# Linear attention and a gated convolution block on one core: four heads' transposes on TensorE, the feature weights on another queue, and a new order list

## The chip, the cores and the metric

The kernel runs on one core of a Trainium2 chip. A core has TensorE (PE in the profile; PEld is its weight load), VectorE (DVE), ScalarE (ACT), GpSimd (POOL) and SyncE (SP). Each engine works through its own queue of instructions in order and waits on semaphores for the others. Transfers are issued from the queues of SP, ACT and POOL and run on 16 DMA engines. The metric is the device time of one execution in microseconds (us); lower is better. The median of three runs before the change is 225.8 us (225.17 to 226.18).

## The reference

There are 8 batches, 8 heads, 576 tokens and 64 numbers per head. Each token's q and k go through the same 64 x 128 matrix `w_phi`, then exp; the attention is linear (keys times values first), and its output runs through a block with a causal depthwise convolution of 5 taps, a sigmoid gate and two 512 x 512 products.

```python
def phi(x):
    proj = np.einsum('bhsd,df->bhsf', x, w_phi)
    proj = proj - np.max(np.abs(proj), axis=-1, keepdims=True)
    return np.concatenate([np.exp(proj), np.exp(-proj)], axis=-1)
q_p, k_p = (phi(q), phi(k))
kv = np.einsum('bhsf,bhsd->bhfd', k_p, v)
z = np.sum(k_p, axis=2)
num = np.einsum('bhsf,bhfd->bhsd', q_p, kv)
den = np.einsum('bhsf,bhf->bhs', q_p, z)[..., None] + 1e-06
...
gate = 1.0 / (1.0 + np.exp(-gate_pre))   # gate_pre: causal convolution of x with conv_w
val = x @ w_val
return (gate * val @ w_out).astype(np.float32)
```

## The kernel before, in words

**Units.** The work is cut into 40 units. Units 0 to 31 are pairs of heads: unit 4b+hp holds heads 2hp and 2hp+1 of batch b, without the last 64 tokens. Units 32 to 39 are the tails: unit 32+b holds the last 64 tokens of all heads of batch b. PSUM has 8 banks, and each operation that writes one names it.

**The order list.** What each engine does, and when, is written out by hand in the string `ORDER` (line 31 on). A word such as `XP.30@5` or `XX.30:A` names an operation, its unit, the PSUM bank after `@` and the engine after `:` (A is ACT, D is DVE, P is POOL). The loop at line 929 calls the function `op_...` of each word in turn, and every engine gets its instructions in that order. So the list sets the order in the five queues, the banks, and for copies the engine too. The words that matter here:

- `LD` (line 364) loads a piece of k, q or v of one batch from POOL's queue; `LD.0` and `LD.1` bring k and q of the second pair of heads of batch 0, `LD.2` and `LD.3` those of the third and fourth. The first pair comes by SP's and ACT's queues (lines 189 to 198), with `w_phi` into the tile `wtmp` between its k and its q.
- `CK`, `CQ`, `W`, `WB` copy that first pair and `w_phi` to bf16 tiles (`W2`, and `W2Z` with zeros beside it).
- `T` (line 368) transposes q and k of a unit on TensorE, `TX` the q half of unit 0; `C` and `CX` copy the result from PSUM to the tile `T`.
- `PK` and `PA` (lines 448, 455) multiply k and q with `w_phi` for the maxima; `MA`, `MB`, `MK`, `MQ` take these maxima on DVE; `KA`, `KB`, `K0`, `K1` take exp of k on ACT (lines 532 and 590). `PQ`, `SA` and `XA`, `XB`, `X0`, `X1` do the same for q, with the maximum subtracted in PSUM by a matmul; `MT` and `MC` turn that maximum round for it.
- `V` scales the values on POOL, `KV` and `KM` form and copy keys times values, `N` and `XN` (lines 686, 713) multiply with q and divide. The result, the tile `XN`, has tokens on the partitions.
- `XP` (line 733) turns `XN` round, channels on the partitions, into the batch's tile `XT`. Without a bank it is a transposing transfer by the crossbar on SP's queue (line 745). With a bank it is four 128 x 128 transposes on TensorE (line 751), and `XX` (line 753) copies them from PSUM to `XT`. The tails always take TensorE.
- `HL` (line 760) copies the four halo planes of `XT` that the convolution reads, `GF` (line 791) is the convolution of a batch on TensorE, `GT` that of its tail, `TH` the tanh, `VA` and `VB` (lines 817, 821) the product with `w_val`, `GV` the gating, `OA` and `OB` (lines 834, 843) the product with `w_out`, `OE` its copy out of PSUM, `ST`, `SL` and `SU` the stores on SP's queue. `FL` is a matmul on zeros whose result nobody reads.

```python
if bank is None:
    nc.sync.dma_start_transpose(
        xt(u.b)[:, u.hp, 4 * 64:12 * 64].rearrange("p (c t) -> p c t", t=P), xf,
    )
else:
    u.XPps = PS[:, bank[0], 0:256].bitcast(BF16)
    for c in range(4):
        nc.tensor.transpose(u.XPps[:, c * P:(c + 1) * P], xf[:, c * P:(c + 1) * P], ident_bf[:, :])
```

Before the change only the last batch (units 28 to 31) has its `XP` with a bank; the other 28 units go by the crossbar.

Of the kernel before, what the change touches and what calls it, by code (L numbers as in the profile page):

```python
# [36 lines left out]
MT.2@4 MC.2:D C.7:D XA.3 T.5@3 C.5:D SA.2 KB.3 E.2 LD.8 V.32:P XA.2 PQ.1@5,4 PA.4@6,7 MQ.4 SA.1 V.2:P PK.4@0,2
MB.4 XB.1 MA.4 T.33@6,7 C.33:D XB.2 KB.4 XA.1 PA.5@3,4 MQ.5 KA.4 KV.1@1 KV.0@7 LD.22 KM.1:D V.3:P LW.0 KM.0:D
PK.33@2,3:W MK.33 MT.4@1 MC.4:D T.6@5 C.6:A N.0@6,7 MQ.33 XN.0 XP.0 N.1@0,1 XN.1 K1.33 K0.33 PK.5@5,4 PA.7@6,7
MQ.7 KB.5 PQ.4@2,3 KA.5 KV.2@0 KM.2:D SA.4 XA.4 MB.5 TP.0@1 CW.0:D E.33 XB.4 N.2@6,7 PQ.33@0,1:W MA.5 KV.3@4  # L40
SA.33 XN.2 XP.2 PK.6@2,5 E.4 XP.1 KM.3:D T.8@6 MT.7@7 MB.6 C.8:D X1.33 X0.33 N.3@3,4 KB.6 XN.3 CV.3:P CV.2:P
XP.3 PK.7@1,0:W MA.7 MC.7:D N.32@6 PA.6@4,5 XN.32 CV.0:P CV.1:P MQ.6 DG.0:P DF.0:P V.33:P KA.6 PQ.7@3,7 SA.7
FL.7@6 V.5:P DF.2:P DF.3:P KA.7 XA.7 XP.32@6 XX.32:D MA.6 DF.1:P T.9@1 C.9:D XB.7 HL.0:P MT.5@4 T.11@6 MC.5:D
KB.7 C.11:D PA.8@2,3 MQ.8 PK.8@1,5:W KA.8 PQ.5@7,4 LD.11 SA.5 XA.5 KV.5@6 MB.7 E.6 XB.5 V.6:P GT.0@2,3 VT.0
KM.5:D MA.8 GF.0@0,1,6,7 HT.0 LD.13 MB.8 LW.1 V.4:P CO.1:P KB.8 TH.1 GW.0 MT.6@4 MC.6:D T.34@2,3 C.34:D TH.0
N.5@4,5 XN.5 XP.5 PK.34@2,3:W PA.9@6,7 K1.34 LD.12 K0.34 MQ.9 PQ.6@4,5 SA.6 V.7:P XB.6 CO.3:P MQ.34 T.10@0
C.10:D PK.9@7,6:W KV.6@1 MK.34 XA.6 MA.9 MT.8@5 KV.4@0 KM.6:A N.6@2,3 MB.9 MC.8:A KM.4:A XN.6 XP.6 N.4@0,1
XN.4 KA.9 XP.4 PQ.8@7,4 PK.10@2,3 KB.9 MA.10 CO.2:A E.8 V.9:P SA.8 V.8:P PA.11@5,6 MQ.11 XA.8 MB.10 VA.2@0
KV.7@1 KM.7:A VB.2 GV.2 VA.3@7 N.7@5,6 XN.7 XP.7 KA.10 XB.8 KB.10 VB.3 GV.3 VA.1@0 LD.14 PA.10@1,2 MQ.10
PK.11@5,6 LD.18 VB.1 GV.1 KB.11 N.33@7 XN.33 PQ.34@3,4 SA.34 VA.0@2 MT.11@1 E.34 X0.34 MC.11:A MB.11 T.13@0  # L50
C.13:D X1.34 KA.11 VB.0 GV.0 T.12@7 C.12:D XP.33@1 XX.33:A LD.16 HL.1:P PQ.11@3,4 SA.11 XA.11 GT.1@0,1 HT.1
MT.9@6 MC.9:D CO.0:P V.34:P MA.11 XB.11 VT.1 E.10 GW.1 V.11:P LD.17 GF.1@2,3,6,7 TH.3 PQ.9@5,4 SA.9 TH.2
PA.12@0,1 XA.9 T.15@6 MQ.12 OA.1@7 PK.12@2,3 KA.12 C.15:D PQ.10@0,1 OB.1 MB.12 XB.9 MT.10@6 V.10:P LD.15
KV.9@5 MC.10:D KM.9:D OE.1:D OA.0@6 SA.10 MA.12 OB.0 KV.8@7 OE.0:D KB.12 KV.11@5 KM.8:D KM.11:D PA.13@2,3
T.35@6,7 N.9@4,5 MQ.13 XN.9 XA.10 XB.10 C.35:A PK.13@0,1 KB.13 PK.35@2,3 MA.13 K0.35 N.8@6,7 XN.8 FL.17@4
FL.18@5 MT.12@4 MC.12:A K1.35 KV.10@5 T.14@4 XP.9 KM.10:A PQ.12@6,7 MB.13 SA.12 MQ.35 MK.35 KA.13 C.14:D
OA.3@5 N.11@0,1 XN.11 N.10@2,3 XN.10 XP.8 XP.11 XP.10 ST.0 XB.12 OB.3 XA.12 OE.3:A PK.15@4,7 PK.14@0,1 KA.14
MA.15 OT.0@6 OF.0:A N.34@5 MA.14 XN.34 PA.15@2,3 OA.2@6 MQ.15 VA.6@0 OB.2 OE.2:D ST.1 KA.15 VB.6 GV.6 MB.14
PQ.35@4,5:W VA.7@2 SA.35 KB.15 E.12 X0.35 X1.35 VA.4@3 VB.7 MT.13@6 MC.13:A VB.4 KB.14 E.35 MB.15 E.14 V.12:P
T.19@0 GV.7 MT.15@4 C.19:D MC.15:D LD.23 GV.4 PQ.13@6,7 SA.13 XA.13 XP.34@2 XB.13 XX.34:D PQ.15@1,0 PA.14@4,5  # L60
MQ.14 SA.15 XA.15 VA.5@3 XB.15 VB.5 LD.19 GV.5 HL.2:P T.16@2 C.16:D GF.2@4,5,6,7 TH.5 PA.16@2,3 GT.2@0,1 TH.4
MQ.16 T.17@6 C.17:D MT.14@7 MC.14:A VT.2 PQ.14@4,3 HT.2 GW.2 PK.16@2,7 PA.17@5,6 KA.16 SA.14 MB.16 MQ.17
OA.5@1 XA.14 OA.4@0 OB.5 V.13:P MA.16 OE.5:D V.14:P OB.4 V.35:P KV.13@6 KM.13:D T.36@4,5 C.36:D T.18@2 KB.16
V.15:P N.13@6,7 C.18:D XN.13 MT.16@5 XB.14 PK.17@4,3 OE.4:A MC.16:A PK.36@0,1 MK.36 KA.17 KV.12@2 XP.13 K0.36
K1.36 OA.7@7 MB.17 LD.25 KV.14@5 OB.7 KM.12:D MA.17 KM.14:A OE.7:A KV.15@2 MQ.36 KM.15:D N.12@4,5 XN.12 KB.17
E.16 PQ.16@1,7 SA.16 XA.16 N.35@6 XP.12 XN.35 N.14@2,3 XB.16 XN.14 ST.2 PQ.36@4,5:W T.20@0 C.20:D SA.36 X0.36
# [10 lines left out]
SA.37 X1.37 X0.37 VA.13@2 VB.14 MT.23@0 MC.23:A GV.14 VB.13 XP.36@6 GV.13 XX.36:D PK.23@7,5 PQ.23@3,4
PA.22@0,1 SA.23 KA.23 MQ.22 MB.23 XA.23 VA.12@2 MA.23 XB.23 OT.1@6 VB.12 GT.4@0,1 GV.12 T.24@3 VT.4 OF.1:D
MT.21@7 KB.23 OA.12@4 T.38@5,6 C.24:D PA.24@2,3 ST.3 E.22 HT.4 MC.21:A GW.4 PQ.21@7,0 MQ.24 SA.21 LD.20 V.20:P
V.37:P V.21:P C.38:A HL.4:P XB.21 OB.12 LD.26 OE.12:D T.25@1 GF.4@2,3,5,6 C.25:D XA.21 TH.9 PK.24@4,0 MA.24  # L80
# [891 lines left out]
```

## Time and profile before

| | before |
|---|---|
| median of the runs | 225.8 us |
| profiled execution, its own time | 226.87 us |
| span of its trace | 225.1 us |
| PE busy | 202.4 us (90%), 3828 matmuls |
| ACT busy | 194.4 us (86%) |
| DVE busy | 184.1 us (82%) |
| POOL busy | 133.4 us (59%) |
| crossbar transposes | 28, all on SP's queue |
| transfers | 31.38 MB, 139 GB/s over the span |

The profiled execution is 1.1 us above the median and 1.8 us above its own span. The views used below: the busy time of each engine in stretches of the span, the chain of waits (followed back from the last instruction, each step to what released it), the timeline of single engines, the groups of instructions by line, and the transfers with their time from issue to landing. The durations of ACT and DVE rows overlap where one instruction follows another closely, so a pair of exps that is 1.1 us long in the timeline moves the chain by 0.98 us.

### The profile page before, as it was taken

To read this page: it belongs to the slowest core of one execution; us is meant where nothing else is said; L and a number is where in the kernel's file an instruction comes from. 1 tells how busy PE (TensorE), PEld (TensorE's weight loads), DVE (VectorE), ACT (ScalarE), POOL (GpSimd) and SP (SyncE) were. 2 spreads that over 40 slices of the span, in tenths; PEclk is the share of its full clock that TensorE was granted. 3 is DMA by queue.
4 is the path that set the end of the run, shared out by engine and by line. 5 is a ranking of instruction groups with operands and counts; after the bars stand their busy time and mean duration, and the time that the engine had idled before them with its cause. 6 is when DMAs were issued, how large, how long until landed. Compare 5 with 4: busy or idle time off the path is not lost.

```text
span 225.1 us, 8971 instructions
## 1 busy us (share of the span) xinstructions
PE 202.4 (90%) x3828; PEld 138.2 (61%) x3854; DVE 184.1 (82%) x337; ACT 194.4 (86%) x425; POOL 133.4 (59%) x172
## 2 busy tenths in 40 slices
PE   0687899996798999999998999999999999999997
PEld 0464677765465665678656775776676666466542
DVE  6499999987886999889996999999988997466341
ACT  3599999998988998999998999999989998777541
POOL 8779967999779702993359509952816086500100
PEclk9997999999999999999999999999999999999999
DMA  5999997699999996984928595796550226304846
GB/s 114 197 199 218 270 203 116 121 204 173 132 167 205 152 147 142 179 141 55 197 50 115 62 203 111 169 136 111 126 114 20 57 47 129 134 4 114 247 105 192
DMA packets 41362, 31.38 MB, mean 139 GB/s; under 512 B 16869, under 2 KB 37349, under 8 KB 41322
## 3 DMA queue, kind: packets, MB, share of 16 engines
q0 software_dynamic: 20816, 14.90, 47.6%
q1 hardware_dynamic: 19882, 15.04, 29.9%
q10 hardware_dynamic: 624, 0.87, 1.2%
q8 instruction: 30, 0.49, 0.9%
q14 instruction: 10, 0.08, 0.1%
HBM read 32.58 MB, written 9.44 MB: 187 GB/s over the span
## 4 chain that ended last, share of the span: by engine, by line
PE 57%; ACT 26%; DVE 9%; issue 3%; DMA 2%; SPq 1%; ACTq 0%; DVEq 0%
PE PS L841 11%; PE PS L812 10%; ACT QT L551 9%; ACT KT L538 8%; PE PS L443 5%; PE PS L706 5%; PE PS L629 4%; PE PS L393 4%; ACT GATE L801 3%; PE PS L652 3%; PE PS L785 3%; PE PS L668 2%; DMA GV<-in_q_dram 2%; DVE MKA L509 2%; PE PS L288 2%
## 5 line engine op out<-in xcount | busy, mean ns | idle before, releaser
L615 POOL TENSOR_TENSOR VT<-vN,EA 128x1024 bf16<-128x1024 bf16 x32 | 61.0, 1907 | 37.2 <-ACT EA L569 30.8
L538 ACT ACTIVATE KT<-PS 128x512 bf16<-128x512 f32 x128 | 70.7, 659 | 2.3 <-PE PS L443 2.2
L551 ACT ACTIVATE QT<-PS 128x512 bf16<-128x512 f32 x128 | 69.2, 657 | 2.8 <-PE PS L668 2.5
L509 DVE TENSOR_REDUCE MKA<-PS 128x4 f32<-128x512 f32 x64 | 42.6, 682 | 1.6 <-ACT KT L538 0.8
L494 DVE TENSOR_REDUCE MQX<-PS 128x8 bf16<-128x1024 f32 x30 | 36.5, 1219 | 4.7 <-PE PS L443 4.4
L812 PE MATMUL PS<-XT,WVAL 128*128 128x512 bf16 x128 | 34.8, 380 | 0.1
L841 PE MATMUL PS<-WOUT,GV 128*128 128x512 bf16 x107 | 30.9, 380 | 1.3 <-issue 0.6
L443 PE MATMUL PS<-W,T 64*128 64x128 bf16 x472 | 24.5, 223 | 4.3 <-ACT T L242 1.8
L828 DVE SCALAR_TENSOR_TENSOR GV<-GATE,PS 128x512 bf16<-128x512 bf16 x32 | 20.9, 680 | 5.3 <-PE PS L812 5.3
L443 PEld LDWEIGHTS <-T 64*128 64x128 bf16 x472 | 15.9, 96 | 12.9 <-issue 6.6
L726 DVE TENSOR_TENSOR XN<-PS,RCPA 128x512 bf16<-128x512 f32 x32 | 22.1, 692 | 1.1
L606 POOL TENSOR_TENSOR VTZ<-vN,EA 64x512 bf16<-64x512 bf16 x16 | 16.6, 1040 | 10.3 <-PE PS L668 6.5
L629 PEld LDWEIGHTS <-KT 128*128 128x128 bf16 x512 | 18.6, 97 | 6.6 <-ACT QT L551 1.2
L629 PE MATMUL PS<-VT,KT 128*128 128x65 bf16 x512 | 21.0, 193 | 1.5 <-ACT QT L551 0.6
L244 POOL COPY XT<-XT 128x1008 bf16<-128x1008 bf16 x8 | 8.2, 1025 | 22.3 <-ACT XT L242 16.1
L706 PEld LDWEIGHTS <-QT 128*128 128x128 bf16 x512 | 18.6, 97 | 4.3 <-issue 0.4
L706 PE MATMUL PS<-KVSA,QT 128*128 128x65 bf16 x512 | 20.6, 193 | 0.1
L244 DVE COPY T<-PS 128x1024 bf16<-128x1024 bf16 x27 | 18.3, 683 | 1.6 <-PE PS L393 1.6
L393 PE MATMUL PS<-ident_bf,kN 128*128 128x128 bf16 x128 | 13.5, 233 | 6.1 <-ACT kN L242 5.5
L801 ACT ACTIVATE GATE<-PS 128x1024 bf16<-128x1024 f32 x16 | 16.0, 1082 | 3.4 <-PE PS L785 3.4
L812 PEld LDWEIGHTS <-WVAL 128*128 128x128 bf16 x128 | 10.5, 97 | 8.4 <-issue 0.6
L852 DVE TENSOR_SCALAR OS<-PS 128x512 f32<-128x512 f32 x16 | 10.9, 685 | 5.5 <-PE PS L841 5.5
(103 smaller groups left out, 371.1 us busy)
## 6 DMA issues: line engine op xcount, KB each, us to landing
out_dram<-OS SPq DMA_DIRECT2D x28, 256.0 KB, 3.6
kN<-in_k_dram POOLq DMA_DIRECT2D x14, 320.0 KB, 7.1
vN<-in_v_dram POOLq DMA_DIRECT2D x14, 320.0 KB, 5.9
qN<-in_q_dram POOLq DMA_DIRECT2D x7, 576.0 KB, 10.8
OS<-in_moe_w_val_dram SPq DMA_DIRECT2D x1, 1024.0 KB, 9.4
out_dram<-OSt SPq DMA_DIRECT2D x8, 128.0 KB, 2.4
vN<-in_v_dram POOLq DMA_DIRECT2D x4, 160.0 KB, 8.0
OS<-in_moe_w_out_dram SPq DMA_DIRECT2D x2, 256.0 KB, 4.4
```

The source lines that it names most:

```text
L244: read(engines[eng].tensor_copy(dst, x), bank)
L443: nc.tensor.matmul(PS[:, bank[par], c0 + blk * P:c0 + (blk + 1) * P], u.T[r, i, blk, :], W2[r, :], start=True, stop=True,)
L494: read(nc.vector.tensor_reduce(MQX[:, i // G % NG, :].rearrange("p (r c) -> p r c", r=2)[:, :, c:c + 4], tokview(u.PA, 0, u, None), AX.X, ...
L509: read(nc.vector.tensor_reduce(out, half_ps(bank, x, out, wide), AX.X, ALU.max, apply_absolute_value=True,), [bank[x]])
L538: read(nc.scalar.activation(out, half_ps(u.PK, x, out, u.PKwide), AF.Exp, scale=1.0 if ft == 0 else -1.0,), [u.PK[x]])
L551: read(nc.scalar.activation(dst, PS[:, u.PQ[x], :].rearrange("p (x t) -> p x t", t=64), AF.Exp, scale=1.0 if ft == 0 else -1.0,), [u.PQ[x]])
L615: e.tensor_tensor(u.VT[:, :, :, 0:D], x.unsqueeze(1).to_broadcast([P, 2, n, D]), w.unsqueeze(3).to_broadcast([P, 2, n, D]), ALU.mult,)
L629: nc.tensor.matmul(PS[:, bank[0], c:c + E1], u.KT[:, ft, j // 2, j % 2, :], u.VT[:, ft, j, :], start=(jj == 0 and x == 0), stop=False, ski ...
L706: nc.tensor.matmul(PS[:, bank[c // 2], x * E1:(x + 1) * E1], u.QT[:, ft, c, h2, :, :].rearrange("p j t -> p (j t)"), kv[:, ft, h2, :], sta ...
L801: read(nc.scalar.activation(m.GATE[q2][:, :, :], banks(*bank), AF.Tanh), bank)
L812: nc.tensor.matmul(PS[:, m.val[jt], :], WVAL[:, dt, jt * P:(jt + 1) * P], planes(xt(m.b), slice(0, P), dt, 4), start=(dt == 0), stop=(dt = ...
L841: nc.tensor.matmul(PS[:, bank, :], lhs(jt), WOUT[:, jt, :], start=(jt == 0), stop=(jt == 3))
```

## The change

Three things change.

1. In the list, `XP.0` to `XP.3` get a bank and `XX.0` to `XX.3` are added: the four pairs of heads of batch 0 are transposed by TensorE and copied to `XT`, one by ACT and three by DVE. 24 crossbar transposes stay.
2. `w_phi` is loaded into `wtmp` from POOL's queue, ahead of everything else there, and no longer from SP's and ACT's queues between k and q of the first pair. On DVE the small tiles made from the identity (`nident`, `ident5`, `id32`) come after the zero fills and no longer between them.
3. The whole list is another one: nearly every word stands elsewhere, and banks differ. Some copies change engine. Of the plain copies out of PSUM, ACT gets six more `OE`, one more `OF`, two more `KM` and the `XX` of two more tails, and loses one `C`, one `CO`, three `MC` and two `XX` of pairs. DVE gets `XX` of six pairs, two `HL`, one `C`, three `MC` and `WB`, and loses six `OE`, one `OF`, two `KM` and two tails' `XX`.

```diff
@@ -29,82 +29,82 @@
 ORDER = """
-LD.0 LD.1 CQ.0:D Z.1:P CK.0:A T.0@5 LD.3 LD.2 W.0:A C.0:A PK.0@0,2 KA.0 TX.0@7 CX.0:A MB.0 T.1@1 C.1:D
...
+CK.0:A T.0@3 WB.0:D LD.1 C.0:D CQ.0:D LD.0 W.0:A PK.0@4,5 KA.0 MB.0 LD.2 LD.3 TX.0@2 CX.0:A LC.0 T.1@6 MA.0
...
@@ -154,6 +154,9 @@
     ctx.enter_context(tc.manual_schedule())
 
+    wtmp = const.tile([P, F], FP32, name="wtmp")
+    for t in range(2):
+        nc.gpsimd.dma_start(wtmp[t * 64:(t + 1) * 64, :], w_phi[:, :])
     ident_bf = const.tile([P, P], BF16, name="ident_bf")
     make_identity(nc, ident_bf[:])
@@ -188,9 +191,6 @@
     W2 = const.tile([P, F], BF16, name="W2")
-    wtmp = const.tile([P, F], FP32, name="wtmp")
-    for t in range(2):
-        (nc.sync, nc.scalar)[t].dma_start(wtmp[t * 64:(t + 1) * 64, :], w_phi[:, :])
     for t in range(2):
@@ -205,14 +205,6 @@
     nc.vector.memset(W2Z[:, :, :].rearrange("p a f -> p (a f)"), 0.0)
-    nc.vector.tensor_scalar_mul(nident[:, :], ident_bf[:, :], -1.0)
-    ident5 = const.tile([5, 5], FP32, name="ident5")
...
@@ -231,6 +223,13 @@
     nc.vector.memset(MQX[:, :, :].rearrange("p g c -> p (g c)"), 0.0)
+    nc.vector.tensor_scalar_mul(nident[:, :], ident_bf[:, :], -1.0)
+    ident5 = const.tile([5, 5], FP32, name="ident5")
...
```

The list's effect is seen in the queues. First POOL's queue at the start of the program, before:

```order
masks.py:199 AFFINE_SELECT ident_bf<-ident_bf 128x128
L178 DMA kN<-in_k_dram 64x2x320 x2
L172 DMA qN<-in_q_dram 128x576
L334 MEMSET OS 128x1
L172 DMA qN<-in_q_dram 128x2x576
L178 DMA kN<-in_k_dram 64x4x320 x2
L244 CAST W2Z<-wtmp 64x128 x2
L178 DMA vN<-in_v_dram 64x4x320 x2
```

and the same place now:

```order
L159 DMA wtmp<-in_w_phi_dram 64x128 x2
masks.py:197 MEMSET ident_bf 128x128
masks.py:199 ISA
masks.py:199 AFFINE_SELECT ident_bf<-ident_bf 128x128
L175 DMA qN<-in_q_dram 128x576
L181 DMA kN<-in_k_dram 64x2x320 x2
L181 DMA kN<-in_k_dram 64x4x320 x2
L175 DMA qN<-in_q_dram 128x2x576
L270 MEMSET VTZ_134 128x1040
L181 DMA vN<-in_v_dram 64x4x320 x2
```

The two transfers of `wtmp` come first, q of the second pair (128x576) passes k of that pair (64x2x320), and k of the third and fourth pair (64x4x320) passes their q. The casts to `W2Z` left POOL for DVE.

Then SP's queue up to the second batch's crossbar transposes, before:

```order
L178 DMA GV<-in_k_dram 64x2x320
L193 DMA wtmp<-in_w_phi_dram 64x128
L195 DMA GV<-in_q_dram 64x576
L291 DMA cw_115<-in_moe_conv_w_dram 5x512
L338 DMA OS<-in_moe_w_val_dram 128x4x512
L745 DMA_TRANSPOSE XT_130<-XN 128x4x128 x4
L343 DMA OS<-in_moe_w_out_dram 32x4x512
L343 DMA OS<-in_moe_w_out_dram 32x2x512 x4
L745 DMA_TRANSPOSE XT_132<-XN 128x4x128 x4
```

and now:

```order
L181 DMA GV<-in_k_dram 64x2x320
L195 DMA GV<-in_q_dram 64x576
L290 DMA cw_115<-in_moe_conv_w_dram 5x512
L337 DMA OS<-in_moe_w_val_dram 128x4x512
L342 DMA OS<-in_moe_w_out_dram 32x4x512
L342 DMA OS<-in_moe_w_out_dram 32x2x512 x4
L744 DMA_TRANSPOSE XT_125<-XN 128x4x128 x4
```

(`GV` is the tile that the first pair's k and q land in; `XT_130` and `XT_123` are the `XT` of batches 0, 2, 4 and 6, `XT_132` and `XT_125` that of the odd ones.) The first four transposes, those of batch 0, are gone from the queue, as is `wtmp`, so that q follows k at once and the load of `w_out` follows that of `w_val`.

Last DVE's queue where batch 0's results are copied into `XT` now:

```order
L725 TENSOR_TENSOR XN<-PS,RCPA 128x512
L243 COPY T<-PS 128x1024
L493 TENSOR_REDUCE MQX<-PS 128x2x4
L243 COPY T<-PS 128x1024
L243 COPY XT_123<-PS 128x512
L508 TENSOR_REDUCE MKA<-PS 128x4
L243 COPY XT_123<-PS 128x512
L243 COPY XT_123<-PS 128x4x64
L243 COPY XT_123<-PS 128x512
```

Three copies of 128x512 stand there that were not in this queue before; the one of 128x4x64 is the tail's and was there.

More of the change, by code (lines that the diff above doesn't have):

```diff
@@ L37 @@
[L37 to L66, printed above, removed]
@@ L77 @@
[L77 to L80, printed above, removed]
-V.22:P OA.13@1 KV.20@7 MB.24 KM.20:D MT.22@5 OB.13 TH.8 V.23:P MC.22:D KV.21@6 PA.25@2,3 OE.13:D KM.21:D MQ.25
@@ L108 @@
+FL.3@4 FL.13@6 FL.10@4 FL.4@3 FL.19@6 FL.21@0 FL.2@2 OE.31:A SL.31
 """
@@ L233 @@
     nc.vector.memset(MQX[:, :, :].rearrange("p g c -> p (g c)"), 0.0)
+    nc.vector.tensor_scalar_mul(nident[:, :], ident_bf[:, :], -1.0)
+    ident5 = const.tile([5, 5], FP32, name="ident5")
+    nc.vector.tensor_copy(ident5[:, :], ident_bf[0:5, 0:5])
+    id32 = const.tile([P, 32], FP32, name="id32")
+    nc.vector.tensor_tensor(id32[:, :], ident_bf[:, 0:32], ident_bf[:, 32:64], ALU.add)
+    nc.vector.tensor_tensor(id32[:, :], id32[:, :], ident_bf[:, 64:96], ALU.add)
+    nc.vector.tensor_tensor(id32[:, :], id32[:, :], ident_bf[:, 96:128], ALU.add)
     MQT = const.tile([P, NG, P], BF16, name="MQT")
```

119 lines of the change are left out of this document (74 added, 45 removed).

## The prediction

> **What bounds the kernel now.** I read the busy time of the engines in stretches first, because the averages of the page (PE 90%, ACT 86%, DVE 82%) hide that different engines are full at different times. Columns: stretch in us, its length, busy us and instructions of PE, PEld, DVE, ACT and POOL, granted clock, transfers' share, GB/s.
>
> ```profile
> core 0: us, PE busy (x) PEld busy (x) DVE busy (x) ACT busy (x) POOL busy (x), PEclk, DMA share, GB/s
> 30.00:35.00 5.00, 4.55 (x104) 3.67 (x102) 4.93 (x12) 5.00 (x11) 1.71 (x4) 1.00 1.30 206
> 35.00:40.00 5.00, 4.60 (x95) 3.66 (x93) 4.90 (x13) 5.00 (x15) 4.77 (x7) 1.00 0.54 79
> 45.00:50.00 5.00, 4.80 (x159) 3.44 (x154) 4.05 (x10) 5.00 (x13) 4.98 (x7) 1.00 1.17 202
> 50.00:55.00 5.00, 3.42 (x78) 2.94 (x74) 3.84 (x7) 4.04 (x10) 5.00 (x6) 1.00 1.30 192
> 55.00:60.00 5.00, 4.56 (x83) 3.22 (x80) 4.82 (x10) 5.00 (x14) 3.37 (x6) 1.00 1.76 147
> 60.00:70.00 10.00, 8.03 (x201) 5.36 (x200) 7.13 (x13) 8.00 (x22) 8.44 (x12) 1.00 1.31 160
> 100.00:110.00 10.00, 9.89 (x225) 7.94 (x226) 9.86 (x22) 9.80 (x23) 5.27 (x7) 1.00 0.68 90
> 110.00:120.00 10.00, 9.95 (x167) 5.99 (x182) 9.77 (x16) 8.59 (x22) 5.13 (x8) 1.00 0.41 83
> 190.00:200.00 10.00, 9.59 (x215) 6.26 (x212) 4.90 (x8) 7.43 (x15) 4.13 (x5) 1.00 0.34 111
> ```
>
> Three stretches follow. At the start the first data and the first copies set the pace (the chain below). In the rows from 30 to 50 us ACT has no idle time and DVE hardly any up to 40, while PE has 0.45 and 0.40 us to spare in five. Later PE is full (9.89 and 9.95 of 10), with ACT close behind. Between the last two, from 50 to 70 us, lies the largest idle time of PE after the start: 1.58 + 0.44 + 1.97 = 3.99 us.
>
> The chain of waits tells what the start hangs on. Columns: start, length, what.
>
> ```profile
> 1.55 0.83 SPq L193
> 2.42 5.33 DMA GV<-in_q_dram
> 7.85 0.47 DVE qN L244
> 8.37 1.48 PE PS L393 x12
> 9.87 0.70 DVE T L244
> ```
>
> The first q is issued behind `w_phi` (0.83 us of SP's queue), lands 5.33 us later, and its copy on DVE, the transposes of q and of unit 1 on PE and the copy of unit 1's result follow without a gap. The timeline names the two longest stalls of PE from 50 to 70 us, by the idle time in brackets and what ended it:
>
> ```profile
> 53.46 0.23 PE L560 MATMUL PS<-ident_bf,MQX 128*128 128x128 bf16 x1 [1.54 <-ACT KVSA L242]
> 61.94 0.46 PE L443 MATMUL PS<-W,T 64*128 64x128 bf16 x10 [1.21 <-issue]
> ```
>
> **The change part by part: the start.** Without `w_phi` between them, q's transfer on SP starts where `w_phi`'s did, 2.42 - 1.55 = 0.87 us sooner, and CQ could run at 6.98. That is the most to win. Against it stands POOL's queue, by these rows (single issues on POOL with their length in ns and their start; PE's first transposes and those of unit 1; time from issue to landing, of the two k pieces and of q behind them):
>
> ```profile
> L178 POOL DMA_DIRECT2D kN<-in_k_dram x1: 776/776/776, 1.4 to 1.4; - x1
> L178 POOL DMA_DIRECT2D kN<-in_k_dram x1: 596/596/596, 2.2 to 2.2; - x1
> 2.80 0.58 POOL L172 DMA_DIRECT2D qN<-in_q_dram  x1
> 5.46 0.61 PE L393 MATMUL PS<-ident_bf,kN 128*128 128x128 bf16 x4 [5.46 <-ACT kN L242]
> ...
> 8.77 0.63 PE L393 MATMUL PS<-ident_bf,kN 128*128 128x128 bf16 x4
> ...
> DMA to landing us min/median/max: 3.6/4.8/5.9
> DMA to landing us min/median/max: 5.8/5.8/5.8
> ```
>
> Two issues for `w_phi`, estimated at the 0.78 + 0.60 of the two for k, and the 0.58 for q now stand ahead of k of the second pair, so its first piece is issued near 1.4 + 1.38 + 0.58 = 3.4 and its second near 4.1 instead of 2.2. With 5.9 us the second lands at 10.0 instead of 8.1; with the 3.6 us of the other piece, at 7.7. Unit 1's transposes, which began at 8.77, need it, and PA.0 and PK.1 are queued behind them on PE; their maxima and exps wait in turn. So the start gains at most 0.87 and loses at most 10.0 - 8.77 = 1.2. The bytes ahead of that piece are the same set as before, only in another order, and the whole set had landed by 2.80 + 5.8 = 8.6; I therefore place unit 1 near 8.4: **-0.4** (ends -0.9 and +1.2). `W` and `WB` need the two `w_phi` transfers, issued near 0.7 and 1.4. With 3.6 to 5.9 us they land between 5.0 and 7.3; the transposes of unit 0 end at 5.46 + 0.61 = 6.1, so this costs nothing up to the middle of that span, and its bad end is inside the +1.2.
>
> **The four transposes.** The group rows and the two queue rows that price them:
>
> ```profile
> L751 PE MATMUL PS<-ident_bf,XN 128*128 128x128 bf16 x16 | 1.5, 219 | 0.0
> L242 ACT ACTIVATE XT<-PS 128x512 bf16<-128x512 bf16 x4 | 2.4, 596 | 0.7 <-PE PS L751 0.5
> L244 DVE COPY Tt<-PS 128x512 bf16<-128x512 bf16 x6 | 2.5, 416 | 0.2 <-PE PS L386 0.2
> 31.98 9.47 SPq L745 DMA_TRANSPOSE XT<-XN  x4
> 44.02 1.02 POOL L244 COPY XT<-XT 128x1008 bf16<-128x1008 bf16 x1
> 44.47 0.74 PE L881 MATMUL PS<-XT,DIAGF 128*128 128x64 bf16 x20
> 38.06 0.69 DVE L726 TENSOR_TENSOR XN<-PS,RCPA 128x512 bf16<-128x512 f32 x1
> ```
>
> PE gets another 16 transposes, 1.5 us busy. They fall between 30 and 45 us, where PE has about 0.4 us idle in five and waits for ACT and DVE: **0** (end +1.5, if that cover is gone). The copies cost ACT 0.60 us and DVE 3 x 0.42 = 1.25 us, in the stretch where both are full. I count the one on ACT, which is full in every row from 30 to 50, and not those on DVE, which has 0.95 us idle right behind, from 45 to 50: **+0.6** (ends 0 and +1.9). What goes is latency: the last division of batch 0 ends at 38.06 + 0.69 = 38.75, its crossbar transposes occupy SP's queue until 41.45, and the halo copy starts at 44.02. By TensorE the same tile is ready near 38.75 + 0.4 + 0.4 = 39.6, some 4 us sooner. PE did not wait for it (the rows of L881 follow without idle time), and the list puts this work behind about as much ACT work as before, so by itself it is worth **0**.
>
> **Copies that change engine.** Their prices, from the groups of instructions:
>
> ```profile
> L850 ACT ACTIVATE OS<-PS 128x512 f32<-128x512 f32 x16 | 9.9, 638 | 3.3 <-PE PS L841 3.3
> L852 DVE TENSOR_SCALAR OS<-PS 128x512 f32<-128x512 f32 x16 | 10.9, 685 | 5.5 <-PE PS L841 5.5
> L242 ACT ACTIVATE MQT<-PS 128x128 bf16<-128x128 bf16 x16 | 5.1, 316 | 2.5 <-PE PS L560 2.4
> ```
>
> Seven output copies move to ACT: 7 x 0.64 = +4.5; three MQT leave: -0.9; the other moves nearly cancel except one T copy and one weight copy less. My total for ACT is about +2.5 us, with batch 0's XX in it; DVE stays within 0.5 us of what it had. Behind 100 us ACT has room (1.41 us between 110 and 120, 2.57 between 190 and 200) and PE is the fuller engine: **0** beyond the 0.6 counted (end +1.9).
>
> **The list.** No row prices a new order. What it can win is PE's idle time, and the two stalls named above, 1.54 and 1.21 us, are of the kind that an order moves: a copy queued behind exps on a full ACT, and a bank that comes free late. SP's queue and `XT` no longer tie batch 0's gate to 44 us, which gives the list PE work to put there. I take one such stall as gone, **-1.4** (ends: +1.4, one more of that size, and -4.0, all of 50 to 70).
>
> **Sum:** -0.4 + 0 + 0.6 + 0 + 0 - 1.4 = -1.2. On the profiled execution, 226.9 us with a span of 225.1, that gives 225.7 and 223.9; the median, 1.1 below it, goes from 225.8 to **224.6**.
>
> **The rivals.**
> - *The list finds more.* If both stalls go and PE's idle time from 60 on shrinks a little, -0.4 + 0.6 - 2.75 - 0.4, near 222.9. For it: four transfers fewer in SP's queue, and data 4 us sooner. Against: from 100 us PE is at 99% already, and its work grows by 1.5.
> - *Nothing comes of it.* Freed latency that nobody waited for: -0.4 + 0.6, 226.0. For it: L881 shows no idle time before it.
> - *Slower by the loads.* The wait for the first q gives way to one for k of the second pair, behind three issues on POOL that were not ahead of it. From a landing later than 8.8 us on, unit 1 is late, and where ACT is full, up to 50 us, such a delay is not caught up: +1.2 + 0.6, 227.6.
> - *Slower by ACT.* If the evictions given to ACT stand where it has no idle time (0.20 us in 10 between 100 and 110), +0.6 + 1.9 - 0.4 = +2.1: 227.9.
> - *Slower by a port.* DVE's zero fills and casts now run while POOL issues `w_phi`. The first of the two k issues above took 0.18 us longer than the second, with DVE's small casts beside it; the longest fill is this:
>
> ```profile
> 2.48 1.12 DVE L227 MEMSET DIAGF<- 128x1280 uint32 x1 [0.19 <-issue]
> ```
>
> If an issue had to wait for a whole fill, 1.1 us would come on top of POOL's queue, and the start would lose 1.1 - 0.4 = 0.7: with the copies +1.3, 227.1. The rule behind this is in the Trainium skill, "SBUF — State Buffer", section "SBUF: two separate sides": transfers issued from GpSimd have their descriptors written by GpSimd, which VectorE locks out while one of its two-port operations runs, and the page advises the other two queues. So it speaks against moving `w_phi`. By the 0.18 us between the two issues the trace agrees at most weakly; no row of it shows a long lock.
> - *That the change does less than it says:* SP's queue in the new order has no transpose ahead of batch 1's, so this has no chance worth a number.
>
> **How the numbers follow.** The sum 0.44, with a range of its own from 223.4 to 225.7; the list finds more 0.18; nothing comes of it 0.15; the loads 0.10; ACT 0.08; the port 0.05. A difference under 0.5%, 1.13 us, cannot be told from none here. Below 224.67 lie 0.26 of the first case and all of the second: faster 0.44. Within 0.5% lie 0.18 of the first, 0.14 of the third and 0.01 of the port: 0.33. The rest, 0.23, is slower. The range for 8 in 10 reaches from the better half of the second case to the loads: 222.3 to 227.5.
>
> **What would show it.** The copy of q (DVE qN) near 7.0 and unit 1's transposes near 8.4 show the start right; transposes at 9.5 or later with the wait put down to the k transfer show the loads. The first halo copy before 42 us shows the latency gone. PE busy from 50 to 70 above 17.4 (16.0 before) shows the term of the list; the same idle time elsewhere shows it wrong. ACT's busy time near 197 us shows the moved copies, and stretches after 100 us with ACT full and PE below 9.5 of 10 would be the fourth rival. A gain that comes after 100 us, where I give none, would make the working wrong even with the right time.

## The result

The changed kernel takes **229.11 us** (median; 229.01 to 229.51) against 225.88 us for the kernel before on the same chip. The ratio is **1.0151**, 95% interval 1.0124 to 1.0178: slower by 3.4 us. In a later set on another chip the same pair gave 1.0127 (1.0086 to 1.0169). The forecast of 224.6 and its range of 222.3 to 227.5 are both wrong.

Times of one kernel spread more in some sets of runs than in others, so below a ratio to the kernel before in the same set is given, without the disturbed runs (six of eleven in experiment 2, five of twelve in experiment 1); a difference in us is that ratio times 225.6 less 225.6.

**The profile after.** Its execution took 229.02 us, with a span of 227.2. First the stretches, with the columns of the prediction:

```profile
core 0: us, PE busy (x) PEld busy (x) DVE busy (x) ACT busy (x) POOL busy (x), PEclk, DMA share, GB/s
45.00:50.00 5.00, 3.18 (x137) 2.71 (x134) 3.19 (x6) 4.19 (x11) 5.00 (x7) 1.00 0.94 206
50.00:55.00 5.00, 4.74 (x118) 3.79 (x102) 4.29 (x8) 4.78 (x9) 4.84 (x8) 1.00 0.91 116
55.00:60.00 5.00, 4.60 (x91) 3.26 (x89) 4.93 (x10) 4.96 (x15) 2.01 (x2) 1.00 0.52 90
60.00:70.00 10.00, 9.79 (x223) 6.86 (x221) 8.30 (x17) 9.63 (x25) 9.64 (x14) 1.00 0.60 74
100.00:110.00 10.00, 9.54 (x207) 7.41 (x209) 8.19 (x18) 8.93 (x23) 3.42 (x5) 1.00 1.18 184
110.00:120.00 10.00, 8.88 (x135) 5.15 (x135) 9.65 (x17) 9.05 (x20) 3.79 (x4) 1.00 0.30 30
```

From 50 to 70 us PE is busy for 4.74 + 4.60 + 9.79 = 19.13 us, where it was 16.01: the stalls that the prediction wanted gone are gone. But from 45 to 50 it has 3.18 instead of 4.80, and from 110 to 120 it has 8.88 instead of 9.95. New idle time stands elsewhere. The groups of instructions say whose it is. Behind the last bar stands the idle time of PE just ahead of the group and what ended it; the first row is of the kernel before, the second of the changed one:

```profile
L892 PE MATMUL PS<-XT,WVAL 128*128 128x64 bf16 x128 | 5.0, 193 | 1.0 <-ACT GATEt L901 0.9
```

```profile
L891 PE MATMUL PS<-XT,WVAL 128*128 128x64 bf16 x128 | 5.0, 193 | 4.3 <-ACT GATEt L900 4.3
```

The group is the operation `VT`: for the last 64 tokens of a batch it multiplies x with `w_val`, 16 matmuls, 0.63 us, in each batch. It has 3.3 us more idle time ahead of it, about what was lost. ACT's `GATEt` is `HT`, the tanh of the same tokens' gate. `GT` (their convolution on PE) fills columns 0 to 127 of two banks, `HT` reads them, and `VT` writes columns 128 to 255 of the same two banks; `GW` on DVE then multiplies both. So `VT` does not need `HT`'s result, yet it waits for it when it stands behind it in the list. Around batch 0 in the timeline of the changed kernel:

```profile
45.69 0.74 PE L880 MATMUL PS<-XT,DIAGF 128*128 128x64 bf16 x20
48.26 0.63 PE L891 MATMUL PS<-XT,WVAL 128*128 128x64 bf16 x16 [1.82 <-ACT GATEt L900]
45.73 2.20 ACT L550 ACTIVATE QT<-PS 128x512 bf16<-128x512 f32 x4
47.64 0.57 ACT L900 ACTIVATE GATEt<-PS 128x256 bf16<-128x256 f32 x1
44.40 1.02 POOL L243 COPY XT<-XT 128x1008 bf16<-128x1008 bf16 x1
```

`GT.0` ends at 46.4. ACT is full and works off four exps first, so `HT.0` begins at 47.64, and PE waits 1.82 us for it with everything that is queued behind. The other waits are 1.00, 0.58, 0.49 and 0.36 us, in batches 3 to 6. The list tells why there are more of them now:

```diff
-GT.0@2,3 VT.0 KM.5:D MA.8 GF.0@0,1,6,7 HT.0
+GT.0@2,3 XB.5 HT.0 VT.0 GW.0 GF.0@0,1,6,7
...
-GT.3@0,1 MQ.20 OE.8:D KA.19 E.18 LD.21 V.17:P V.19:P SA.17 VT.3 HT.3
+GT.3@4,5 HT.3 C.21:D VT.3
```

Before, `HT` stood ahead of `VT` in three of eight batches (1, 5, 7); now it does in seven, all but batch 2.

The start came out nearly as forecast (copy of q, PE's first transposes of unit 1):

```profile
6.64 0.46 DVE L243 CAST qN<-GV 128x576 bf16<-128x576 f32 x1
8.57 0.59 PE L392 MATMUL PS<-ident_bf,kN 128*128 128x128 bf16 x4 [0.76 <-DMA kN<-in_k_dram]
```

and the end is later than before. PE's last output matmuls and the last of ACT's four output copies:

```profile
217.84 3.62 PE L840 MATMUL PS<-WOUT,GV 128*128 128x512 bf16 x16
221.20 0.50 ACTq L861 DMA_DIRECT2D out_dram<-OS  x1
222.92 0.60 ACT L849 ACTIVATE OS<-PS 128x512 f32<-128x512 f32 x1 [0.58 <-ACT OS L849]
```

All four copies of the last outputs (`OE.28` to `OE.31`) are on ACT, with the issue of a store between them; in the kernel before, `OE.31` was on DVE.

### The profile page after: what moved, and what is told of

It reads as the page before. It is cut to its first block, busy times and chain, and to the rows that moved or that the text cites. A ratio compares the mean times of both kernels' runs of the same rounds, so it can differ in the third digit from the quotient of the medians.

```text
span 227.2 us, 8980 instructions
## 1 busy us (share of the span) xinstructions
PE 202.8 (89%) x3845; PEld 138.4 (61%) x3870; DVE 184.4 (81%) x340; ACT 195.4 (86%) x429; POOL 132.7 (58%) x171
## 4 chain that ended last, share of the span: by engine, by line
PE 46%; ACT 34%; DVE 12%; issue 4%; DMA 2%; POOL 1%; ACTq 0%; POOLq 0%
ACT KT L537 12%; ACT QT L550 12%; PE PS L840 9%; PE PS L811 7%; PE PS L784 4%; PE PS L442 4%; PE PS L392 3%; PE PS L705 3%; PE PS L628 3%; PE PS L651 3%; DVE MQX L493 2%; DVE XN L725 2%; PE PS L891 2%; PE PS L667 2%; DMA kN<-in_k_dram 2%
## 5 line engine op out<-in xcount | busy, mean ns | idle before, releaser
L537 ACT ACTIVATE KT<-PS 128x512 bf16<-128x512 f32 x128 | 71.6, 689 | 4.0 <-PE PS L442 3.3
L550 ACT ACTIVATE QT<-PS 128x512 bf16<-128x512 f32 x128 | 68.5, 650 | 3.1 <-PE PS L667 2.8
L243 DVE COPY T<-PS 128x1024 bf16<-128x1024 bf16 (+1 forms) x28 | 18.8, 674 | 4.2 <-PE PS L392 4.0
L849 ACT ACTIVATE OS<-PS 128x512 f32<-128x512 f32 x22 | 13.7, 636 | 3.8 <-PE PS L840 3.2
L392 PEld LDWEIGHTS <-kN 128*128 128x128 bf16 x128 | 9.5, 104 | 11.9 <-ACT kN L241 5.5
L840 PEld LDWEIGHTS <-GV 128*128 128x128 bf16 x128 | 10.4, 98 | 9.5 <-issue 1.4
```

The source lines that it names most:

```text
L392: nc.tensor.transpose(u.Tps[:, x, blk, :], a, ident_bf[:, :])
L537: read(nc.scalar.activation(out, half_ps(u.PK, x, out, u.PKwide), AF.Exp, scale=1.0 if ft == 0 else -1.0,), [u.PK[x]])
L550: read(nc.scalar.activation(dst, PS[:, u.PQ[x], :].rearrange("p (x t) -> p x t", t=64), AF.Exp, scale=1.0 if ft == 0 else -1.0,), [u.PQ[x]])
L840: nc.tensor.matmul(PS[:, bank, :], lhs(jt), WOUT[:, jt, :], start=(jt == 0), stop=(jt == 3))
```

## The experiments

**1. The start alone** (`e1_wphi_only`): the kernel before with the second part of the change, the first lines of which are

```diff
+    wtmp = const.tile([P, F], FP32, name="wtmp")
+    for t in range(2):
+        nc.gpsimd.dma_start(wtmp[t * 64:(t + 1) * 64, :], w_phi[:, :])
     ident_bf = const.tile([P, P], BF16, name="ident_bf")
```

> The kernel before with one part of the change: the transfers of w_phi stand first on POOL's queue and the small DVE setup behind the zero fills; list as before. In the changed kernel qN was copied at 6.64 us against 7.85 and unit 1's transposes began at 8.57 against 8.77. Theory 1 (the loss lies in the order of the list, not in this part): 225.4 to 225.9, equal or up to 0.4 us faster. Rival (POOL's queue is the loss, since the second k pair waits behind three issues): 1 to 2 us slower, 227 to 228, with unit 1's transposes waiting for the k transfer.

Measured: 0.9972 (0.9937 to 1.0007), -0.6 us. The start is not the loss; the interval holds a gain like the forecast one and no change.

**2. The transposes alone** (`e2_xp_only`), put into the list before:

```diff
-KA.5 KV.2@0 KM.2:D
+KA.5 XP.0@1 KV.2@0 KM.2:D XX.0:A
...
-XN.32
+XN.32 XX.3:D
```

> The kernel before with the other named part alone: the four heads of batch 0 transposed by TensorE, each result copied out (the first by ACT, three by DVE), nothing else moved. Theory 1 (the 16 transposes and four copies lie where PE has time to spare, 30 to 45 us): 225.4 to 226.6. Rival A (PE's total work decides, and it grows by 1.5 us): 227.2 to 227.5, about half of the loss. Rival B (the halo copy 4 us sooner is worth something): below 225.2.

Measured: 1.0088 (1.0047 to 1.0129), +2.0 us, the size of rival A. But the trace names another reason than PE's work. PE waited for the two banks that I had taken:

```profile
34.98 0.41 PE L290 MATMUL PS<-ident,cw 5*128 5x5 f32 x4 [0.80 <-ACT XT L237]
41.84 0.37 PE L647 MATMUL PS<-T,W 64*128 64x512 bf16 x1 [0.51 <-DVE XT L239]
```

**3. The order of two words** (`e3_vt_first`), in the changed kernel:

```diff
-GT.0@2,3 XB.5 HT.0 VT.0 GW.0
+GT.0@2,3 XB.5 VT.0 HT.0 GW.0
...
-GT.3@4,5 HT.3 C.21:D VT.3
+GT.3@4,5 VT.3 HT.3 C.21:D
```

and so in every batch but 2.

> The changed kernel with one thing moved: for each batch the value matmuls of the last 64 tokens (VT) stand ahead of the tanh of their gate (HT), which reads the same two banks, and not behind it. In the changed kernel PE stood idle 4.3 us ahead of VT for that tanh, 1.0 us in the kernel before. Theory 2 (this wait is a main part of the loss): the idle time ahead of VT falls below 0.5 us and the time by 1.5 to 3.3 us, to 225.8 to 227.6. Rival (PE would only wait for the same ACT work a few instructions later): 228.7 to 229.3.

Measured: 0.9991 (0.9962 to 1.0020), so 3.1 to 3.6 us faster than the changed kernel by its two ratios, 1.0127 and 1.0151. The idle time ahead of the group is gone:

```profile
L886 PE MATMUL PS<-XT,WVAL 128*128 128x64 bf16 x128 | 5.0, 193 | 0.0
```

Theory 2 holds: with this order put back the loss against the kernel before is gone, within an interval from 0.9 us faster to 0.5 us slower. PE does not just wait a little later for the same ACT work.

**4. The last output copy on DVE** (`e4_last_on_dve`), in the changed kernel: `OE.31:A` becomes `OE.31:D`.

> The changed kernel with the very last eviction (OE.31) on DVE as in the kernel before, not on ACT. In the changed kernel ACT does all four last evictions, with the issue of a store between each two (0.60 and 0.50 us in turn), and the last one starts at 222.92, where PE's last output matmul ended at 221.46. Theory 3 (the end is 1.4 us late because ACT's queue alternates): 1.0 to 1.5 us faster, 227.6 to 228.1. Rival (the stores behind it on SP's queue end last anyway): 228.8 to 229.3.

Measured: 1.0103 (1.0069 to 1.0136). Against 1.0151 this looks like the 1.1 us that I expected, but the profile does not bear it out. Its span is 0.9 us shorter, and 0.7 of that is there at the first halo copy (43.67 against 44.40 in the changed kernel), long ahead of the edit. The two executions differ in the clock granted to PE from 20 to 25 us, 0.66 in the changed kernel's and 1.00 in this one (the last section has the rows); behind it this one is 0.55 us ahead (24.68 against 25.23 for the same matmuls). From PE's last output matmul to the end of the span it is 226.3 - 220.77 = 5.5 us, and 227.2 - 221.46 = 5.7 before the edit:

```profile
43.67 1.02 POOL L238 COPY XT<-XT 128x1008 bf16<-128x1008 bf16 x1
...
217.15 3.62 PE L835 MATMUL PS<-WOUT,GV 128*128 128x512 bf16 x16
220.81 0.69 DVE L846 TENSOR_SCALAR OS<-PS 128x512 f32<-128x512 f32 x1 [2.87 <-DMA out_dram<-OSt]
221.06 0.60 ACT L844 ACTIVATE OS<-PS 128x512 f32<-128x512 f32 x1 [0.58 <-PE PS L835]
221.69 1.37 ACTq L856 DMA_DIRECT2D out_dram<-OS  x2
```

ACT's own third copy now ends last (221.66) and its last store is issued behind it. By the profile the edit gives 0.2 us; theory 3 falls. In the same set this kernel, which keeps `HT` ahead of `VT`, is about 2.5 us slower than that of experiment 3.

**5. Both repairs** (`e6_vt_first_last_dve`): experiments 3 and 4 in one kernel.

> The changed kernel with both repairs: value matmuls of the last 64 tokens ahead of the tanh of their gate in every batch, and the last eviction on DVE. Alone they gave 3.5 and 1.1 us. If they are two separate losses they add up: 224.1 to 224.8, and with that the new list is faster than the kernel before by about 0.5%. If both are the same time at the end: 225.0 to 225.6.

Measured: 0.9981 (0.9948 to 1.0013), the same as experiment 3 within the intervals. The two do not add up, as the 0.2 us says.

**6. The opposite move** (`e7_before_ht_first`), in the kernel before: in batches 0, 2, 3, 4 and 6 `VT` goes right behind `HT`.

```diff
-GT.0@2,3 VT.0 KM.5:D MA.8 GF.0@0,1,6,7 HT.0
+GT.0@2,3 KM.5:D MA.8 GF.0@0,1,6,7 HT.0 VT.0
```

> The kernel before with the opposite move: in batches 0, 2, 3, 4 and 6, where VT stands ahead of HT, it is put right behind it. Theory 2 (PE waits for the tanh that ACT reaches late, and the time is not made up): idle time of PE ahead of VT from 1.0 to 3 or more, the time 1.5 to 3.5 us longer, 227.2 to 229.2. Rival (other work of the changed list made that wait long; here ACT gets to the tanh in time): below 226.4.

Measured: 1.0090 (1.0053 to 1.0127), +2.0 us. The time agrees with theory 2, the idle time ahead of the group does not: it rose only from 1.0 to 1.4 us. Its group, then batch 4 in its timeline, then the row of the kernel before that answers to the last one:

```profile
L887 PE MATMUL PS<-XT,WVAL 128*128 128x64 bf16 x128 | 5.0, 193 | 1.4 <-ACT GATEt L896 1.2
```

```profile
143.37 0.42 DVE L902 SCALAR_TENSOR_TENSOR GVt<-GATEt,PS 128x256 bf16<-128x256 bf16 x1 [1.14 <-PE PS L887]
144.48 2.07 ACT L546 ACTIVATE QT<-PS 128x512 bf16<-128x512 f32 x4 [1.82 <-PE PS L663]
```

```profile
144.20 2.06 ACT L551 ACTIVATE QT<-PS 128x512 bf16<-128x512 f32 x4 [0.30 <-PE PS L668]
```

Here a later `VT` made DVE wait 1.14 us for its product, and ACT 1.82 us for PE's work behind it, where it had waited 0.30. A delayed instruction is paid by whoever is queued behind those who wait for it. That is one place; where all of the 2.0 us go was not added up.

**7. The changed kernel with the crossbar again** (`e5_after_xbar`, and `e8_e6_crossbar` with both repairs as well):

```diff
-XP.1@6 PA.8@2,3 XX.1:D XP.32@5
+XP.1 PA.8@2,3 XP.32@5
```

and so for the other three heads.

> The changed kernel with the heads of batch 0 back on SP's crossbar and their four copies out of the banks left out; the rest of the list, with the value matmuls behind the tanh, as in the changed kernel. In the kernel before, putting those 16 transposes and copies in cost 2 us, of which 1.3 were waits for two banks that I had chosen (0.80 and 0.51 us ahead of the next user). Theory 4 (the transposes and copies cost their own PE and copy time, 0.6 to 1.5 us, in any list): 227.5 to 228.4. Rival (the searched list hides them): 228.8 to 229.3, or later if the halo copy now waits for SP's queue.

> The changed kernel with both repairs and with batch 0's heads on the crossbar again. If the transposes by TensorE cost 0.6 to 1.5 us in this list too: 222.8 to 224.0, the fastest so far. If the list hides them: the same as with both repairs, 224.1 to 224.8. If SP's queue makes the halo copy of batch 0 late in this list: above 225.

Measured: 1.0402 (1.0368 to 1.0437) and 1.0261 (1.0233 to 1.0289), +9.1 and +5.9 us. The expectations had the direction, a halo copy kept late by SP's queue, but nothing of this size. The second one's trace shows a place that I had not looked at. The words `XP.1` and `XP.2` stand behind `LW.1`, the transfers of `w_out` on SP's queue, so the two transposing transfers were issued at 46.18, landed near 51.3, and PE stood still:

```profile
43.45 2.69 SPq L337 DMA_DIRECT2D OS<-in_moe_w_out_dram  x6
46.18 2.50 SPq L739 DMA_TRANSPOSE XT<-XN  x2
51.30 0.96 PE L875 MATMUL PS<-XT,DIAGF 128*128 128x64 bf16 x15 [6.38 <-DMA XT<-XN]
```

The two kernels tell of that place, not of the crossbar.

**8. The crossbar in a good place** (`f1_e6_crossbar_early`): both repairs, and each `XP.0` to `XP.3` right behind its division, ahead of `LW.1`.

```diff
-N.0@1,2 XN.0 KA.4
+N.0@1,2 XN.0 XP.0 KA.4
```

> The changed kernel with both repairs, and batch 0's heads on SP's crossbar, each right behind its division, so ahead of the transfer of the output weights, which held SP's queue from 43.4 to 46.2 us in the two kernels that came out at 231 and 234 us; their four copies left out. Theory 4 (the transposes by TensorE cost 0.6 to 1.5 us in any list): 223.7 to 224.7. Rival A (this list hides them): 225.0 to 225.6. Rival B (the crossbar itself is late for this list, wherever it stands): above 226, with PE idle behind 44 us for XT.

Measured: 0.9973 (0.9939 to 1.0006), against 0.9981 with TensorE's transposes. In the new list the two ways differ by 0.2 us, give or take about 1 us by the two intervals. That is rival A's number, but the 0.6 us at the low end of theory 4 is not excluded.

**9. Other banks in the list before** (`f2_xp_other_banks`): as experiment 2, with `XP.0@3`, `XP.1@6`, `XP.2@3`, `XP.3@5`, later in the list, all four copies on DVE, and `N.32` in bank 7.

> The kernel before with batch 0's heads transposed by TensorE once more, now with banks that nobody needs soon, each later in the list and all four copies on DVE. The first such kernel was 2.0 us slower and showed 0.80 and 0.51 us of PE waiting for my two banks. Theory 4 (own price of 0.6 to 1.5 us): 226.2 to 227.0, and no wait for these copies in the trace. Rival A (only the bank waits cost): 225.4 to 226.0. Rival B (the price is 2 us or more whatever the banks): 227.3 or more.

Measured: 1.0154 (1.0099 to 1.0209), +3.5 us. Rival B by its number, and again by waits that I had put there:

```profile
36.68 0.38 PE L746 MATMUL PS<-ident_bf,XN 128*128 128x128 bf16 x4 [1.51 <-ACT QT L546]
41.52 0.45 PE L690 MATMUL PS<-KVSA,QTt 128*64 128x65 bf16 x16 [1.18 <-DVE MQT L239]
```

The first is `XP.0` waiting for bank 3, which an exp on the full ACT reads; the second is `N.32` waiting for bank 7. Between 30 and 45 us a bank that is free in the list is still to be read by an engine that is behind. So the transposes' own price was not measured in the old list; what both tries show is that banks which they took were still in use.

**10. Two repairs of the kernel before** (`f3_before_wphi_vt_first`): experiment 1, and `VT` ahead of `HT` in batches 1, 5 and 7.

> The kernel before with w_phi's transfers first on POOL's queue and with the value matmuls ahead of the tanh in batches 1, 5 and 7 too, where PE waited 0.76 and 0.16 us; the crossbar and the rest of the list as before. If the gains of the start (0.6 us) and of these waits (0.9 us) add up: 224.0 to 224.6. If PE waits for ACT a little later instead: 224.8 to 225.4.

Measured: 1.0023 (0.9988 to 1.0057). Neither gain shows, though the idle time ahead of `VT` is gone. The trace tells where a gain of the start went. A `PQ` that ran at 55.74 in the kernel before runs at 54.14, 1.6 us sooner, but then PE waits for the k of batch 3, which POOL issued no sooner (51.96 against 51.79) and which took longer to land (10.0 us against 8.7 in the median of two pieces):

```profile
63.48 0.38 PE L387 MATMUL PS<-ident_bf,kN 128*128 128x128 bf16 x4 [2.09 <-DMA kN<-in_k_dram]
```

These transposes ran at 64.18 before. Behind the wait the clock granted to PE falls to 0.50, and at 71 us this kernel is 0.2 us behind the one before (71.23 against 71.00). Experiment 1's trace has the same wait, 1.23 us, and is at 71.24. So in these two executions a load around 63 us stood in the way of what had been won ahead of it. Why the waits taken out of batches 5 and 7 bring nothing is not shown.

**11. Which batches** (`f4_vt0_first`: `VT` ahead of `HT` in batch 0 alone; `g1_vt_first_1to7`: in the others; `g4_change_again`: the changed kernel beside them).

> The changed kernel with the value matmuls ahead of the tanh in batch 0 alone, where PE's idle time ahead of them was 1.82 us of the 4.3; in the other batches as in the changed kernel. If each wait costs its own length up to the end: 1.3 to 1.8 us faster, 227.3 to 227.8, with the other half left to batches 3 to 7. If a loss at 48 us is caught up in the slack up to 70 us: 228.6 to 229.2.

> The changed kernel with the value matmuls ahead of the tanh in batches 1 to 7, and behind it in batch 0 alone: the complement of the run that moved batch 0 and gained 1.8 us. Waits of 1.00 + 0.58 + 0.49 + 0.36 us go, 2.4 in all. If each wait costs its own length: 226.5 to 227.2. If those after 110 us, where all engines are full, cost more than their length because ACT and DVE run dry behind them too: 225.4 to 226.4. If they cost less: above 227.8.

> The changed kernel itself once more, so that the others of this set stand beside it on the same chip: 228.7 to 229.6, with 4.0 to 4.5 us of PE idle ahead of the value matmuls of the last 64 tokens.

Measured: 1.0077 (1.0042 to 1.0111), 1.0068 (1.0038 to 1.0097) and 1.0127 (1.0086 to 1.0169). By the changed kernel's two ratios batch 0 is worth 1.1 to 1.7 us and the other six 1.3 to 1.9, against idle times of 1.82 and 2.43. Their traces keep 2.4 and 1.8 us of the idle time, that of the batches not moved. Together the two gains make 2.5 to 3.5 us, near the 3.1 to 3.6 of experiment 3: each group of waits costs 0.5 to 0.9 of its length, early or late alike. The slack that the list had made from 50 to 70 us was not there to catch up the first one.

**12. A bank of its own** (`g2_vt_own_bank`): the changed list as it is, and `VT` writes all four parts into a third bank.

```diff
-                    PS[:, m.tb[x], 128 + s * 64:192 + s * 64], WVAL[:, dt, jt * P:(jt + 1) * P],
+                    PS[:, m.vb, jt * 64:jt * 64 + 64], WVAL[:, dt, jt * P:(jt + 1) * P],
```

> The changed kernel with its list as it is, tanh ahead of the value matmuls, but the value matmuls write into a bank of their own (one bank that is free at that place, for all four parts) and not into the other half of the two banks that the tanh reads. Theory 2a (PE waits only because both share a bank): the idle time put down to the tanh goes to nothing and the time to 225.2 to 226.2, as with the order changed. Rival (the wait stands for something else, such as XT or the gate's matmuls coming late): the idle time stays near 4 us and the time above 228.5.

Measured: 1.0153 (1.0110 to 1.0196), as slow as the changed kernel, though the wait for the tanh is gone: 0.8 us is left ahead of `VT`, 0.6 of it for an exp that read the third bank. The waits of PE by their releaser (line, in us, times, longest) show where it went:

```profile
PE PS L779 <- DVE GVt L901: 1.4, 3, 0.8
PE PS L646 <- DVE GVt L901: 0.7, 1, 0.7
PE PS L387 <- DVE GVt L901: 0.6, 1, 0.6
PE PS L886 <- ACT QT L545: 0.6, 1, 0.6
```

The next users of the third bank waited 2.7 us for `GW`, and that for the same tanh. Both halves of theory 2a are answered: the wait is one of a shared bank, but a bank of its own did not bring the time back. In five of eight batches the very next work of PE uses the third bank that I had picked (behind `VT.0@1` and `GW.0` comes `GF.0@0,1,6,7`), and those five are the first three rows. Whether a bank with a later user would do better was not tried. The Trainium skill, "PSUM — Partial Sum Buffer", section "PSUM bank collisions raise a hardware error", says that two engines must not touch the same bank in the same 32 partitions at once, at other columns either, and that the compiler therefore makes one wait for the other. The traces agree: 4.3 us of waiting between columns 0 to 127 and 128 to 255 of one bank, and none for the tanh with separate banks. That an actual overlap would do harm was not tried, and the traces do not tell which part of the software sets the wait here.

**13. What is left to gain** (`g3_best`): experiment 8 with `OE.30` on DVE too and ACT's store issues behind its own copies.

> The changed kernel with the value matmuls ahead of the tanh, batch 0's heads on the crossbar right behind their divisions, and the last two of four output evictions on DVE with ACT's store issues behind its own evictions. The end from PE's last output matmul to the end of the span was 5.7 us with all four on ACT, 5.5 with the last on DVE, 5.1 in the kernel before. If it comes to 5.1 or less here: 224.0 to 224.8, faster than the kernel before by 0.4 to 0.7%. If the stores on the queues set the end: 224.8 to 225.4.

Measured: 0.9949 (0.9920 to 0.9978), 224.55 us against 225.59 of the kernel before in that set: faster than both. PE's last output matmuls and the last copy:

```profile
213.30 3.62 PE L835 MATMUL PS<-WOUT,GV 128*128 128x512 bf16 x16
216.95 0.69 DVE L846 TENSOR_SCALAR OS<-PS 128x512 f32<-128x512 f32 x1 [0.60 <-PE PS L835]
```

From 216.92 to the end of the span, 222.3, it is 5.4 us, so the end gave 0.3 of the gain and not the 0.6 hoped for.

## Why the prediction was wrong

- **The list, -1.4: the step that failed.** The mechanism was half right. The stalls from 50 to 70 us went, and PE's 19.13 us passed the mark of 17.4 that I had set. But I counted what a new order takes away and not what it brings. Its end of +1.4, one more stall of that size, was too small: five waits of PE for `GATEt` came, 4.3 us against 1.0 before, and moving two words per batch gives the time back (experiment 3). With that order mended the kernel is at 0.9991, so the list's gain and the price of what it carries about cancel: with the prediction's own -0.4 and +0.6 for start and copies, the measured -0.2 us leaves -0.4 for the list, give or take 0.7, not -1.4. Where the rest of the gain from 50 to 70 us goes was not found. And the row of the second of the two stalls, 1.21 us, named no releaser (`issue`), so that a late bank caused it was a guess. The prediction said that the same idle time elsewhere would show this term wrong; it does.
- **It could have been read in the order.** Both lists and the two banks stood in the code, the 0.9 us of waiting for `GATEt` was in the trace of before, and `HT` ahead of `VT` went from three batches to seven. I compared places that the diff spoke of, and not every pair that shares a bank.
- **The start, -0.4: right in its landmarks, not settled in its price.** CQ at 6.64 (forecast 6.98), unit 1 at 8.57 (8.4), with a wait of 0.76 us for the k piece, less than the end of that range. Alone it measured -0.6 us, with an interval up to +0.2, so the rivals of the loads (+1.2) and of the port (+0.7) are out for the start. Later a load did take the gain back in the old list (10), which the prediction had not seen.
- **The transposes, 0, and their copies, +0.6: not contradicted here, but the reason was wrong.** In the new list TensorE and crossbar differ by 0.2 us, with an uncertainty of about 1 us (5 and 8). I named PE's spare time from 30 to 45 us as the cover. In the old list, with that spare time, they cost 2.0 and 3.5 us, of which 1.3 and 2.7 us are waits for banks in the rows above; my ends for PE time and copies were +1.5 and +1.9.
- **Crossbar latency, 0: right, but its sign did not come.** The first halo copy was to start before 42 us. It started at 44.40, no sooner than the 44.02 of before. In the new list the last heads' transposes and copies end only at 43.91, and POOL, which makes the halo copy, is busy with its own earlier work until 44.3. In the kernel before POOL came to the halo copy without idle time too, so by these rows it did not wait for the crossbar, and its start was no sign of the latency. The new list's rows:

```profile
42.75 0.40 PE L750 MATMUL PS<-ident_bf,XN 128*128 128x128 bf16 x4
42.97 0.94 DVE L243 COPY XT<-PS 128x512 bf16<-128x512 bf16 x3
43.46 0.72 POOL L243 COPY DIAGF<-DIAG 32x640 bf16<-32x640 bf16 x1
44.24 0.10 POOL L333 MEMSET OS<- 128x1 f32 x1
```

- **Copies that change engine, 0: right as far as seen.** ACT's busy time is 195.4 us, 1.0 more than before (forecast 2.5 more, near 197). The one part tested, the last copy on ACT, costs 0.2 us.
- **The rivals.** "Slower by ACT" gave 227.9 and asked for PE below 9.5 of 10 behind 100 us; PE is at 8.88 from 110 to 120, but ACT, which was to be full, is at 9.05. The number was near by luck: ACT is in it, but its mechanism, evictions where ACT has no idle time, is not what was found. None of the rivals named an order of two engines on one bank.

What stays open: the own price of the transposes in a list with banks to spare; where the new list, with its order mended, loses most of what it wins from 50 to 70 us; and why the waits in batches 5 and 7 of the kernel before cost nothing (10) where those of the changed list cost most of their length.

## What to carry to other kernels

When an order list is made anew, compare old and new for every pair of instructions on two engines that share a bank (or another resource that only one may hold): who comes first, and how full is the engine that is waited for. A producer that needs nothing of the other belongs ahead of a reader on the fuller engine; in the kernel before, where a load held PE up nearby, that move brought nothing (10). In the profile of after, sort the groups by idle time ahead of them and by releaser before looking at the named edits: one row held the 3.3 us here. And an edit that is put into a finished list by hand measures the hand's choice of banks and queue places first.
